# Column-tiled dense matmuls beside PV, V expanded by DMA, and joined ln/exp in a fused attention and token-mixer kernel

## The chip, the cores and the metric

The kernel runs on one core of one Trainium2 chip. The metric is device time in microseconds (us), the median of several executions. "PE" is the matmul engine, "PEld" its weight loads, "DVE" the vector engine, "ACT" the scalar (activation) engine, "POOL" the general engine, "SP" the engine that issues DMAs. The times of one kernel lie within about 1% of each other. So a difference of 2 us between two kernels is near the edge of what these runs can tell.

## The reference

Two layers. Each is attention with a sliding window of 256 over 2,048 tokens with 32 heads of 16 elements, then a mixer that multiplies along the tokens.

```python
# attention: B=1, S=2048, D=512, H=32, Dh=16, W=256
q, k, v = split(layernorm(x) @ wqkv)
scores = einsum("bhqd,bhkd->bhqk", q, k) * Dh ** -0.5
p = softmax(where(0 <= q_idx - k_idx < 256, scores, -1e9))
x = x + (p @ v merged over the heads) @ wo
# token mixer: F=1792
u = gelu(einsum("bsd,sf->bdf", layernorm(x), w1) + b1)     # u is [D, F]
x = x + (einsum("bdf,fs->bds", u, w2) + b2) transposed
# both once more with the same weights
```

## The kernel before

The program builds a graph of operations. A small list scheduler with assumed costs orders them for each engine, at build time; the chip then runs five fixed instruction streams that wait for each other on semaphores.

Scores ("sc") take 32 of PE's 128 rows for each of four heads. PV takes 32 of PE's columns for each of four groups of heads. Everything else (projections, output projection, both halves of the mixer) is "dense", on the whole array; V's projection uses 64-column tiles. Dense groups ("fillers", class "f") are put between scores and PV, so that PE has work while ACT takes the exp.

```python
LAT = {...}; SWITCH = 95.0            # assumed cost of a change of tiling on PE
def _rank(self, o, now, ready):       # who goes first on PE among those that can start
    ...
    if o.cls == "sc":   k = 0
    elif o.cls == "pv": k = 1 if self.cfg in ("sc", "pv") or now - ready[o.idx] > 2500 else 3
    else:               k = 2         # fillers
    return (k, o.prio, o.idx)

# PSUM: 3 pairs of banks for scores, and 2 single banks
psum2 = Pool("psum2", 3)
psum  = Pool("psum", 2)
psum.classes = {"od": [0, 1], "f": [0, 2]}   # od: what PV sums into; f: fillers

# a dense group: matmuls into one bank, which DVE then copies out
def proj(o, which):
    ft = filler(wide)
    mm_group(ft, 4, lambda e, c: e.matmul(bank(ft), lhsT=wqkv[:, c, ...], rhs=xhT[:, tx.slot, c, :], ...))
    op("vector", lambda e: e.tensor_copy(qT[...] or stg[...], bank(ft)), ...)

# V: projection in 64-column tiles, copy by DVE, expansion to block-diagonal form by POOL
for h in range(2):
    op("gpsimd", lambda e, h=h: e.tensor_scalar(vbd[:, tk.slot, 2*sp:2*sp+2, :, 16*h:16*h+16],
       stg[...], half[:, h:h+1], 0.0, op0=ALU.mult, op1=ALU.add), ...)

# attention: scores -> exp (ACT) -> mask (DVE) -> PV (PE) -> denominators
last = e.matmul(bank(t)[32*r:32*r+32, ...], lhsT=onesbd[:] if den else vbd[:, tk.slot, jj, 4*o + r, :],
                rhs=pt[:, tp.slot, r, ...], tile_position=(0, 32*r), ...)
# per group of 8 heads: DVE copies out, ACT takes exp(-ln(denominator)), POOL multiplies
op("scalar", lambda e: e.activation(rl[:, tr.slot, 1, :], rl[:, tr.slot, 1, :], ACTF.Ln), ...)              # 256 columns
op("scalar", lambda e: e.activation(rl[:, tr.slot, 1, :], rl[:, tr.slot, 1, :], ACTF.Exp, scale=-1.0), ...)
```

The softmax here doesn't subtract the row's maximum and nothing guards it: scores larger than these inputs give would overflow.

Of the kernel before, what the change touches and what calls it, by code (L numbers as in the profile page):

```python
# [6 lines left out]
dt = mybir.dt  # L7
ALU = mybir.AluOpType
# [27 lines left out]
class Op:  # L36
    __slots__ = ("idx", "eng", "fn", "cost", "lat", "prio", "deps", "users", "ndeps", "tiles", "start", "end",
                 "done", "seq", "dma", "extra", "cfg", "cls")


class Graph:
# [13 lines left out]
    def op(self, eng, fn, reads=(), writes=(), cost=100.0, lat=None, prio=None, dma=False, after=(), holds=(),  # L55
           cfg=None, cls=None):
# [5 lines left out]
        o.cfg, o.cls = cfg, cls  # L62
# [80 lines left out]
    LAT = {"tensor": 205.0, "vector": 125.0, "scalar": 155.0, "gpsimd": 95.0, "sync": 0.0}  # L143
    SWITCH = 95.0

    def _rank(self, o, now, ready):
        if o.cls is None:
            return (0, o.prio if o.prio is not None else o.idx, o.idx)

        if o.cls == "sc":  # L150
            k = 0
        elif o.cls == "pv":
            k = 1 if self.cfg in ("sc", "pv") or now - ready[o.idx] > 2500 else 3
        else:
            k = 2
        return (k, o.prio, o.idx)

    def schedule(self):
        self.cfg = None
# [4 lines left out]
        dma_free = 0.0  # L164
# [5 lines left out]
        while left:  # L170
            best = None
            for e in self.ENGS:
                m = INF
                ests = []
                for o in cand[e]:
                    t = max(ready[o.idx], free[e])
                    if any(tl.slots is None for tl in o.tiles):
                        t = max(t, self._alloc_time(o))
                    ests.append(t)
                    if t < m:  # L180
                        m = t
# [9 lines left out]
            if o.dma:  # L191
                free[e] = m + 600.0
# [3 lines left out]
            else:  # L196
                if e == "tensor":
                    if o.cfg != self.cfg:
                        o.cost += self.SWITCH
                    self.cfg = o.cfg  # L200
                o.end = free[e] = m + o.cost
                o.done = o.end + o.lat
# [12 lines left out]
    def emit(self, block):  # L215
# [60 lines left out]
        for e in self.ENGS:  # L276
            def body(eng, e=e):
                for o in self.order[e]:
                    for s, v in waits[o.idx]:
                        eng.wait_ge(sem(s), v)  # L280
                    ins = o.fn(eng)
# [47 lines left out]
def bass_interleave_layers__sliding_block__mixer_token_mlp__prompt_kernel(  # L329
# [22 lines left out]
    with es:  # L352
# [9 lines left out]
        vbd = sb("vbd", [P, 3, 8, 16, 32])  # L362
        pt = sb("pt", [P, NPT, 4, 512])
        rl = sb("rl", [P, 4, 2, 256], dt.float32)
# [28 lines left out]
        p_kv, p_pt, p_rl, p_oT = Pool("kv", 3), Pool("pt", NPT), Pool("rl", 4), Pool("oT", 3)  # L393
# [66 lines left out]

        def ln_stats(t):
# [5 lines left out]
        def ln_block(t, twice):  # L467
# [9 lines left out]
               reads=[f"x{t}", f"ag{t}", f"rs{t}"], writes=[f"xh{t}"], cost=dve_cost(512, 0.25, ptrs=2))  # L477
# [9 lines left out]

        def mm_group(dst, n, mk, reads, cols=512, step=2, prio=None, holds=(), after=()):

            prio = fprio() if prio is None else prio  # L490
            for k0 in range(0, n, step):
                k1 = min(n, k0 + step)

                def f(e, k0=k0, k1=k1):
                    last = None
                    for k in range(k0, k1):
                        last = mk(e, k)
# [3 lines left out]
                   cls="f")  # L501


        def qkv(m, wide0):
            tx, tq, tk = Tile(p_xhT), Tile(p_qT), Tile(p_kv)
            wide = wide0
            for i in range(4):
                t = 4 * m + i
                if not wide:
                    op("sync", lambda e, i=i, t=t: e.dma_start_transpose(xhT[:, tx.slot, :, i * P:(i + 1) * P],  # L510
                                                                         xh_sb[:, t, :]),
                       reads=[f"xh{t}"], writes=[(tx, i)], dma=True, cost=900, prio=-1e5)
# [17 lines left out]
            def proj(o, which):  # L530
                ft = filler(wide)
                ts = Tile(p_stg) if which else None
                mm_group(ft, 4, lambda e, c: e.matmul(  # L533
                    bank(ft), lhsT=wqkv[:, c, which * 512 + o * P:which * 512 + (o + 1) * P],
                    rhs=xhT[:, tx.slot, c, :], start=(c == 0), stop=(c == 3)), XT + [f"w{which}"],
# [7 lines left out]
                for h in range(2):  # L543
                    op("gpsimd", lambda e, h=h: e.tensor_scalar(  # L544
                        kbd[:, tk.slot, o, :, h, :], stg[:, ts.slot, :].rearrange("p (s n) -> p s n", n=64),
                        par[:, h:h + 1], 0.0, op0=ALU.mult, op1=ALU.add),
                       reads=[ts, ("par", h)], writes=[(tk, "k", o, h)], cost=pool_cost(512, 1))

            def vproj(sp):
                ft, ts = filler(wide), Tile(p_stg)  # L550
                for k0 in range(0, 4, 2):
                    def f_v(e, k0=k0):
                        last = None
                        for c in range(k0, k0 + 2):
                            for sc in range(2):
                                tok = (2 * sp + sc) * 64
                                for hf in range(2):
                                    last = e.matmul(
                                        bank(ft)[64 * hf:64 * hf + 64, sc * 256:(sc + 1) * 256],
                                        lhsT=xhT[:, tx.slot, c, tok:tok + 64],  # L560
                                        rhs=wqkv[:, c, 1024:1536].rearrange("p (r h e) -> p r h e", h=2, e=16)[:, :, hf, :],
                                        start=(c == 0 and sc == 0), stop=(c == 3), tile_position=(0, 64 * hf),
                                        skip_group_check=True)
                        return last
                    op("tensor", f_v, reads=[(tx, sp), "w2"], writes=[ft], cost=mm_cost(4, 256),
                       prio=fprio(), holds=[ts, tk], cfg="v", cls="f")
                op("vector", lambda e: e.tensor_copy(stg[:, ts.slot, :], bank(ft)),  # L567
                   reads=[ft], writes=[ts], cost=dve_cost(512, psum=True), prio=-2e5)
                for h in range(2):
                    op("gpsimd", lambda e, h=h: e.tensor_scalar(  # L570
                        vbd[:, tk.slot, 2 * sp:2 * sp + 2, :, 16 * h:16 * h + 16],
                        stg[:, ts.slot, :].rearrange("p (s r e) -> p s r e", s=2, e=16), half[:, h:h + 1], 0.0,
                        op0=ALU.mult, op1=ALU.add),
# [17 lines left out]
        def attention(c, tqs, tks):  # L591
# [6 lines left out]
            for o2 in range(0, 4, 2):  # L598
# [3 lines left out]
                od = {}  # L602
                left = {o2: nb, o2 + 1: nb}
                for su in order:
# [3 lines left out]
                    def f_sc(e, su=su, tt=(tA, tB)):  # L608
                        last = None
                        for k, o, base in su:  # L610
                            for j, q0, n, c0 in plan[k][0]:
                                tk, jj = blk(j)
                                for r in range(4):
                                    last = e.matmul(  # L614
                                        PS[:, 2 * tt[r // 2].slot + r % 2, base + c0 * 64:base + (c0 + n) * 64],
                                        lhsT=kbd[32 * r:32 * r + 32, tk.slot, o, jj, :, :].rearrange("p h n -> p (h n)"),
# [8 lines left out]
                    prev_sc[0] = op("tensor", f_sc, reads=rd, writes=[tA, tB], cost=cols / 2.4 + 15,  # L625
# [7 lines left out]
                    for c0, nc_, w0 in plan[su[0][0]][1]:  # L633
# [8 lines left out]
                        op("vector", f_mask, reads=keys + LD, writes=keys, cost=dve_cost(4 * n * nc_ * 64, 0.5))  # L642
                    for k, o, base in su:
# [4 lines left out]
                        def f_pv(e, k=k, o=o, base=base, tp=tp, first=first, t=od[o]):  # L648
                            last, st = None, first
                            for j, q0, n, c0 in plan[k][0]:  # L650
                                tk, jj = blk(j)
                                for den in (0, 1):
                                    for r in range(4):
                                        last = e.matmul(  # L654
                                            bank(t)[32 * r:32 * r + 32, den * 256 + q0 * 64:den * 256 + (q0 + n) * 64],
                                            lhsT=onesbd[:] if den else vbd[:, tk.slot, jj, 4 * o + r, :],
# [8 lines left out]
                        op("tensor", f_pv, reads=keys + rd, writes=[od[o]], cost=plan[k][2] * 128 / 2.4 + 15,  # L665
# [4 lines left out]
                        t, tr = od[o], Tile(p_rl)  # L670
                        op("vector", lambda e, t=t, tr=tr: e.tensor_copy(  # L671
# [183 lines left out]
```

## Time and profile before

| | before |
|---|---|
| time | 504.44 us (503.77 to 505.47, 4 runs) |
| span of the profiled run, granted clock of PE | 503.9 us, 0.996 |
| PE / DVE / ACT / POOL busy | 94% / 71% / 68% / 40% |
| attention of layer 1, first to last exp of the scores | 16.7 to 181.9 us |
| attention of layer 2 | 230.7 to 412.0 us |

The busy share is a mean over stages. The last 92 us, after the last exp, are dense matmuls alone.

Groups of instructions of the kernel before that the change touches (busy us, mean ns of one, then idle time before them and what ended it):

```profile
L676 ACT ACTIVATE rl<-rl 128x256 f32<-128x256 f32 x64 | 29.5, 461 | 0.3
L674 ACT ACTIVATE rl<-rl 128x256 f32<-128x256 f32 x64 | 29.3, 458 | 11.2 <-DVE rl L671 11.0
L654 PEld LDWEIGHTS PS<-pt,vbd 128*32 128x32 bf16 x1920 | 44.1, 96 | 39.3 <-DVE pt L638 14.2 <-issue 5.7 <-DVE agg L464 3.2
L654 PE MATMUL PS<-pt,vbd 128*32 128x64 bf16 x480 | 17.0, 199 | 0.7 <-DVE pt L640 0.6
```

### The profile page before, as it was taken

To read this page: it belongs to the slowest core of one execution; us is meant where nothing else is said; L and a number is where in the kernel's file an instruction comes from. 1 tells how busy PE (TensorE), PEld (TensorE's weight loads), DVE (VectorE), ACT (ScalarE), POOL (GpSimd) and SP (SyncE) were. 2 spreads that over 40 slices of the span, in tenths; PEclk is the share of its full clock that TensorE was granted. 3 is DMA by queue.
4 is the path that set the end of the run, shared out by engine and by line. 5 is a ranking of instruction groups with operands and counts; after the bars stand their busy time and mean duration, and the time that the engine had idled before them with its cause. 6 is when DMAs were issued, how large, how long until landed. Compare 5 with 4: busy or idle time off the path is not lost.

```text
span 503.9 us, 16930 instructions
## 1 busy us (share of the span) xinstructions
PE 471.2 (94%) x7584; PEld 231.2 (46%) x7584; DVE 357.8 (71%) x715; ACT 342.6 (68%) x464; POOL 202.0 (40%) x330
## 2 busy tenths in 40 slices
PE   3977989999999999999999999999989899999997
PEld 1553445545444444453454445344544444444443
DVE  6898998887867755477778878887888685342222
ACT  1597999999999964404993999399979980330000
POOL 3797876666213221036427535643655131000000
PEclk9998999999999999999999999999999999999999
DMA  8411120330131377410030034700100239534163
GB/s 266 80 34 34 24 34 3 84 88 3 44 86 46 86 187 198 113 38 12 3 97 12 14 86 96 178 3 14 23 2 3 77 107 255 142 100 140 56 197 102
DMA packets 81689, 39.89 MB, mean 79 GB/s; under 512 B 18128, under 2 KB 81616, under 8 KB 81616
## 3 DMA queue, kind: packets, MB, share of 16 engines
q1 hardware_dynamic: 81616, 38.81, 29.3%
q8 instruction: 59, 0.97, 0.8%
q14 instruction: 14, 0.11, 0.1%
HBM read 33.56 MB, written 2.10 MB: 71 GB/s over the span
## 4 chain that ended last, share of the span: by engine, by line
PE 45%; ACT 31%; DVE 18%; POOL 4%; issue 1%; DMA 1%
ACT pt L628 27%; PE PS L780 16%; PE PS L754 10%; PE PS L740 5%; PE PS L654 5%; DVE pt L638 3%; PE PS L533 3%; PE PS L614 3%; DVE stats L462 3%; PE PS L687 2%; DVE xh_sb L475 2%; ACT rl L674 2%; DVE stg L567 2%; ACT rl L676 2%; DVE qT L538 2%; DVE rl L671 1%
## 5 line engine op out<-in xcount | busy, mean ns | idle before, releaser
L628 ACT ACTIVATE pt<-PS 128x1024 bf16<-128x1024 f32 (+1 forms) x304 | 295.3, 1058 | 55.4 <-PE PS L614 54.5
L638 DVE TENSOR_TENSOR pt<-pt,ldm 128x512 bf16<-128x512 bf16 (+1 forms) x192 | 77.0, 401 | 24.9 <-ACT pt L628 23.1
L654 PE MATMUL PS<-pt,vbd 128*32 128x64 bf16 (+3 forms) x1920 | 82.8, 237 | 7.1 <-DVE pt L638 4.7
L678 POOL TENSOR_TENSOR oT<-rl 128x256 bf16<-128x256 f32 x64 | 48.1, 751 | 91.7 <-ACT rl L676 91.1
L654 PE MATMUL PS<-pt,onesbd 128*32 128x64 bf16 (+3 forms) x1920 | 81.8, 233 | 0.0
L533 PE MATMUL PS<-xhT,wqkv 128*128 128x512 bf16 x256 | 67.0, 392 | 2.8 <-DVE stg L541 0.9
L780 PE MATMUL PS<-uT,w2b 128*128 128x512 bf16 x280 | 65.8, 380 | 0.8 <-DVE rl L671 0.8
L614 PE MATMUL PS<-qT,kbd 32*128 32x64 bf16 (+3 forms) x1920 | 60.6, 232 | 4.1 <-ACT pt L628 2.3
L544 POOL TENSOR_SCALAR kbd<-stg,par 128x512 bf16<-128x512 bf16 x64 | 51.2, 811 | 27.6 <-DVE stg L541 23.8
L654 PEld LDWEIGHTS PS<-pt,vbd 128*32 128x32 bf16 x1920 | 44.1, 96 | 39.3 <-DVE pt L638 14.2
L740 PE MATMUL PS<-xh_sb,w1b 128*128 128x512 bf16 x224 | 55.1, 381 | 1.7 <-DVE w2b L744 0.8
L570 POOL TENSOR_SCALAR vbd<-stg,half 128x512 bf16<-128x512 bf16 x64 | 50.4, 799 | 13.1 <-DVE stg L567 8.4
L614 PEld LDWEIGHTS PS<-qT,kbd 32*128 32x128 bf16 x1920 | 27.6, 93 | 57.5 <-ACT pt L628 37.6
L785 DVE SCALAR_TENSOR_TENSOR x_sb<-PS,b2col,x_sb 128x512 bf16<-128x512 f32 x32 | 24.0, 749 | 39.7 <-PE PS L780 39.7
L754 PE MATMUL PS<-xh_sb,w1b 128*128 128x512 bf16 x224 | 49.2, 379 | 0.8 <-DVE x_sb L690 0.8
L770 ACT ACTIVATE uT<-rl,b1col 128x512 bf16<-128x512 f32 x28 | 18.4, 712 | 44.5 <-DVE rl L764 44.5
L471 POOL TENSOR_SCALAR rstd<-agg 128x1 f32<-128x1 f32 x64 | 13.6, 213 | 82.7 <-DVE agg L464 79.9
L654 PEld LDWEIGHTS PS<-pt,onesbd 128*32 128x32 bf16 x1920 | 45.8, 97 | 0.1
L671 DVE COPY rl<-PS 128x512 f32<-128x512 f32 x64 | 43.6, 681 | 2.9 <-PE PS L654 2.3
L462 DVE BATCH_NORM_STATS2 stats<-x_sb 128x6 f32<-128x512 bf16 x64 | 43.7, 686 | 1.3 <-DMA x_sb<-in_A_x_dram 0.4
L473 POOL TENSOR_TENSOR rstd<-rstd,mhalf 128x1 f32<-128x1 f32 x64 | 39.0, 610 | 3.8
L475 DVE TENSOR_SCALAR xh_sb<-x_sb,agg,rstd 128x512 bf16<-128x512 bf16 x64 | 32.9, 515 | 10.4 <-POOL rstd L473 9.6
(45 smaller groups left out, 487.6 us busy)
## 6 DMA issues: line engine op xcount, KB each, us to landing
w1b<-in_B_w_dram SPq DMA_DIRECT2D x28, 512.0 KB, 4.7
w2b<-in_B_w_dram SPq DMA_DIRECT2D x10, 896.0 KB, 5.2
pt<-in_B_w_dram SPq DMA_DIRECT2D x12, 448.0 KB, 6.5
out_dram<-x_sb SPq DMA_DIRECT2D x16, 128.0 KB, 1.8
wqkv<-in_A_wqkv_dram SPq DMA_DIRECT2D x3, 512.0 KB, 6.2
x_sb<-in_A_x_dram SPq DMA_DIRECT2D x3, 512.0 KB, 8.8
x_sb<-in_A_x_dram SPq DMA_DIRECT2D x2, 256.0 KB, 3.0
wo_sb<-in_A_wo_dram SPq DMA_DIRECT2D x1, 512.0 KB, 8.9
```

The lines of the kernel that those rows point to most:

```text
L462: op("vector", lambda e: e.bn_stats(stats[:, t, :], x_sb[:, t, :]), reads=[f"x{t}"], writes=[f"st{t}"], cost=dve_cost(512))
L533: mm_group(ft, 4, lambda e, c: e.matmul(bank(ft), lhsT=wqkv[:, c, which * 512 + o * P:which * 512 + (o + 1) * P], rhs=xhT[:, tx.slot, c, : ...
L544: op("gpsimd", lambda e, h=h: e.tensor_scalar(kbd[:, tk.slot, o, :, h, :], stg[:, ts.slot, :].rearrange("p (s n) -> p s n", n=64), par[:, ...
L570: op("gpsimd", lambda e, h=h: e.tensor_scalar(vbd[:, tk.slot, 2 * sp:2 * sp + 2, :, 16 * h:16 * h + 16], stg[:, ts.slot, :].rearrange("p ( ...
L614: last = e.matmul(PS[:, 2 * tt[r // 2].slot + r % 2, base + c0 * 64:base + (c0 + n) * 64], lhsT=kbd[32 * r:32 * r + 32, tk.slot, o, jj, :, ...
L628: op("scalar", lambda e, ts=ts, tp=tp, i=i, cols=cols: e.activation(pt[:, tp.slot, 2 * i:2 * i + 2, 0:cols], PS[:, 2 * ts.slot:2 * ts.slot ...
L638: return e.tensor_tensor(v, v, msk.unsqueeze(1).to_broadcast([P, 4, w]), op=ALU.mult)
L654: last = e.matmul(bank(t)[32 * r:32 * r + 32, den * 256 + q0 * 64:den * 256 + (q0 + n) * 64], lhsT=onesbd[:] if den else vbd[:, tk.slot, j ...
L671: op("vector", lambda e, t=t, tr=tr: e.tensor_copy(rl[:, tr.slot].rearrange("p a b -> p (a b)"), bank(t)), reads=[t], writes=[tr], cost=dv ...
L740: mm_group(ft, 8, lambda e, sc, tt=tt, ft=ft: e.matmul(bank(ft), lhsT=w1b[:, tw.slot, sc, tt * P:(tt + 1) * P], rhs=xh_sb[:, sc, :], start ...
L754: last = e.matmul(PS[:, 2 * tu.slot + tt, :], lhsT=w1b[:, tw.slot, sc - 8, tt * P:(tt + 1) * P], rhs=xh_sb[:, sc, :], start=(sc == 8), sto ...
L780: mm_group(ft, NFT, lambda e, fc: e.matmul(bank(ft), lhsT=w(fc)[:, k * P:(k + 1) * P], rhs=uT[:, fc, :], start=(fc == 0), stop=(fc == NFT ...
```

## The change

PE should change its tiling less often, ACT should do fewer instructions, POOL should lose most of V's expansion. The core of the diff:

```diff
# 1. dense matmuls next to sc or pv become four 32-column tiles; V's projection too (cfg "v" -> "pv")
+        def matmul(e, cols32, o, w, x, start, stop):
+            if not cols32:
+                return e.matmul(o, lhsT=w, rhs=x, start=start, stop=stop, skip_group_check=True)
+            for j in range(0, P, 32):
+                last = e.matmul(o[j:j + 32], lhsT=w[:, j:j + 32], rhs=x, start=start, stop=stop,
+                                tile_position=(0, j), skip_group_check=True)
+            return last
+                    if o.flex and self.cfg in ("sc", "pv"):      # in the scheduler
+                        o.cfg = "pv"
# 2. V: columns of one head 16 elements apart, so that a DMA moves runs of 512 bytes; zeroed once by POOL
+        for i in (1, 2):
+            op("gpsimd", lambda e, i=i: e.memset(<vbd slot i, 128x4096 bf16 as 128x2048 f32>, 0.0), ...)
+                        op("sync", lambda e, h=h: e.dma_start(<vbd half h>, <stg half h>), ...)   # 48 of 64
-  lhsT=onesbd[:] if den else vbd[:, tk.slot, jj, 4 * o + r, :],
+  lhsT=onesbd[:] if den else vbd[:, tk.slot, jj, 4 * o + r::16],
# 3. ln and exp of the denominators once for two groups of heads
-                        op("scalar", ... rl[:, tr.slot, 1, :] ... Ln)      # 256 columns, 64 times; Exp the same
+                        for fn, sc in ((ACTF.Ln, 1.0), (ACTF.Exp, -1.0)):
+                            op("scalar", ... rl[:, tr.slot, 1] ...)        # 512 columns, 32 times each
# 4. a new order: rank of PV, more costs in the scheduler's model
-            k = 1 if self.cfg in ("sc", "pv") or now - ready[o.idx] > 2500 else 3
+            k = 1 if self.last == "pv" or now - ready[o.idx] > 2500 else 3
... (in the scheduler's model: lock of the port that DVE and POOL share, cold clock at the start, issue time of DMAs;
     also 3 rl buffers of twice the size in place of 4, and the last output projection of a layer in a single bank)
```

A reason for the strided weights in 2: a version that read two runs of 16 columns did not build.

## The prediction

> **What bounds it now.** The page gives PE 94% busy, DVE 71%, ACT 68%, POOL 40% of 503.9 us. The chain of waits names ACT (31%, mostly the scores' exp) between 80 and 165 us and between 327 and 410 us, but I do not take it for the limit. After each stretch PE still works off dense matmuls that did not fit (first-half w1 until 180 and 428 us, then 24 us of w1 and 48 us of w2 at 216 ns per 512-column matmul). So the time is PE's work plus PE's lost time. From the timeline's start times: streaming all columns at 2.4 GHz, four at a time where 32-wide tiles are used, needs about 398 us. The other 106 us are lost, about 95 of them between groups of different tiling. There are some 450 changes of group (score rows, PV columns, V columns, dense), median 115 to 140 ns above streaming each: about 55 us. The other 40 us are waits, 12 of them between 20 and 80 us (windows: DVE 19 of each 20 us, POOL up to 19).
>
> The Trainium skill (TensorEngine Tiling (Array Packing), Key Properties) says that changing the tiling mode drains the engine; the 115 to 140 ns at each change agree.
>
> **What the change does.**
> 1. Dense matmuls next to PV, and V's projection, use PV's column tiling, so PV-dense and PV-V changes no longer drain. What stays is about two changes for each of the 152 score groups, some 300 in place of 450: 150 x 125 ns, about -18 us, all on PE. Four 32-wide matmuls should stream like one dense one: PV's four 256-column matmuls already start every 109 ns. They lose fast weight load (same page), but PV's weight loads hide at this pitch. I allow +3 us.
> 2. 48 of 64 V expansions (799 ns) leave POOL: -38 us of 202, plus 4 for zeroing. They become 48 small DMAs of about 2 to 3 us with slack, since K and V are made a block ahead. The chain is little on POOL (4%): perhaps -4 us of PE waits, early and between 225 and 325 us.
> 3. 128 ln/exp of 256 columns (458 and 461 ns) become 64 of 512, about 670 ns (256 columns more at 0.83 ns): ACT -16 us of 343. ACT being half hidden, -3 us of PE waits.
> 4. The new order lets fillers run ahead of PV: fewer waits behind exp and mask, -3 us. Strided V weights and V copy cost +1 us.
>
> Sum: -18 + 3 - 4 - 3 - 3 + 1 = -24 us: **480 us**, range 467 to 493. Faster by over 2%: 0.84; within 2%: 0.12; slower: 0.04.
>
> **What would show it.** PE starts after PV-dense changes at streaming pitch, with about 300 drains of 115 to 140 ns left; dense matmuls of 32 columns four to about 216 ns; POOL near 165 us; ln and exp 32 each near 670 ns; ACT near 327 us; the last 72 us unchanged; the gain spread over 20 to 428 us.
>
> **What would make it wrong.** Column-tiled dense matmuls slower than 216 ns for four (weight loads showing): 740 groups x 30 ns would eat all. The V DMA stuck behind transposes on its in-order queue, so that PV waits. PV delayed so long that the probability buffers run out and ACT stalls. A much slower strided V copy on DVE, which is full between 20 and 60 us. The other way: more of the 40 us of waits gone.

## More of the kernel before

The page of the kernel before: busy time by engine, the instruction queue, and the chain of waits (the work that ended last, followed backwards), by engine and by line. L628 is the exp of the scores.

```profile
PE 471.2 (94%) x7584; PEld 231.2 (46%) x7584; DVE 357.8 (71%) x715; ACT 342.6 (68%) x464; POOL 202.0 (40%) x330
...
q8 instruction: 59, 0.97, 0.8%
...
PE 45%; ACT 31%; DVE 18%; POOL 4%; issue 1%; DMA 1%
ACT pt L628 27%; PE PS L780 16%; PE PS L754 10%; PE PS L740 5%; PE PS L654 5%; DVE pt L638 3%; PE PS L533 3%; PE PS L614 3%; DVE stats L462 3%; PE PS L687 2%; DVE xh_sb L475 2%; ACT rl L674 2%; DVE stg L567 2%; ACT rl L676 2%; DVE qT L538 2%; DVE rl L671 1%
```

PE is the busiest engine, but the chain runs through ACT for 31% of the span. Two stretches of the kernel before in the windows view (start and end, length, then busy us of PE, PEld, DVE, ACT and POOL with counts, granted clock, DMA share, GB/s):

```profile
56.00:140.00 84.00, 79.81 (x1785) 41.53 (x1786) 72.49 (x142) 81.66 (x109) 51.96 (x75) 1.00 0.18 42
140.00:180.00 40.00, 39.44 (x856) 19.27 (x852) 29.36 (x60) 40.00 (x56) 9.34 (x16) 1.00 0.23 66
```

Between 140 and 180 us ACT never pauses (40.00 of 40.00 us) and PE is busy 39.44. But in the 124 us of these two lines ACT is idle for 84.00 − 81.66 = 2.34 us in all. At this order, and with the same work on ACT, nothing that is done to PE can make this stretch shorter by more. In layer 2 it is different: between 231 and 410 us the same view leaves ACT idle for 22.7 us.

## The result

| | before | after |
|---|---|---|
| time | 504.44 us (503.77 to 505.47, 4 runs) | 510.14 us (507.39 to 510.57, 4 runs) |
| profiled span, granted clock | 503.9 us, 0.996 | 508.4 us, 0.993 |
| first matmul | 6.8 us | 9.3 us |
| attention of layer 1 (first to last exp) | 165.2 us long | 167.9 us long |
| attention of layer 2 | 181.2 us long | 180.9 us long |

The ratio after to before is 1.010, with a 95% interval of 1.006 to 1.014. Here and below a ratio is the mean time of one kernel's runs over that of the other's in the same rounds, so it is not quite the ratio of the medians. The change costs 1%, where 24 us of gain were predicted. The page of the kernel after, the same lines (L662 is the scores' exp; L510 are the column-tiled dense matmuls, L508 and L791 the others):

```profile
PE 464.8 (91%) x10334; PEld 252.7 (50%) x10334; DVE 357.2 (70%) x715; ACT 337.4 (66%) x400; POOL 168.3 (33%) x284
...
q8 instruction: 81, 1.33, 1.0%
...
PE 55%; ACT 23%; DVE 19%; issue 1%; POOL 1%; POOLq 0%
ACT pt L662 22%; PE PS L510 17%; PE PS L508 13%; PE PS L791 9%; PE PS L689 8%; PE PS L648 4%; PE PS L582 3%; DVE stats L479 3%; DVE pt L672 3%; DVE xh_sb L492 2%; DVE rl L706 2%; DVE pt L674 2%; ACT rl L712 2%; DVE stg L591 2%; DVE x_sb L728 2%
```

POOL lost what was predicted (202.0 to 168.3 us), but ACT only 5 us and not 16, and PE went from 7,584 to 10,334 matmuls. The windows view of the kernel after, the same two stretches of time (not quite the same work):

```profile
56.00:140.00 84.00, 77.69 (x2360) 46.09 (x2360) 70.05 (x141) 80.80 (x94) 36.40 (x54) 1.00 0.24 55
140.00:180.00 40.00, 38.35 (x1112) 21.14 (x1108) 28.73 (x59) 39.83 (x48) 8.83 (x15) 1.00 0.25 70
```

PE's busy time fell from 39.44 to 38.35 us in the second stretch. ACT is still at 39.83 of 40. The groups of the kernel after:

```profile
L689 PEld LDWEIGHTS PS<-pt,vbd 128*32 128x32 bf16 x1920 | 64.7, 139 | 26.9 <-DVE pt L672 6.3 <-DVE pt L674 3.3 <-issue 2.5
L712 ACT ACTIVATE rl<-rl 128x512 f32<-128x512 f32 x64 | 42.2, 659 | 15.1 <-DVE rl L706 14.9
L689 PE MATMUL PS<-pt,vbd 128*32 128x64 bf16 x480 | 19.8, 223 | 2.3 <-DVE pt L674 1.1 <-DVE uT L781 0.4 <-DVE x_sb L728 0.4
```

### A ledger of PE

From the start times of all matmuls: streaming every column at 2.4 GHz, four tiles at a time where tiles are used, needs 398 us in both kernels. What lies between first and last matmul beyond that is lost time. I count a gap at a change of tiling as a drain of about 105 ns and what is beyond (over 150 ns) as a wait.

| us | before | after |
|---|---|---|
| first to last matmul | 493.5 | 495.6 |
| changes of tiling | 466 | 307 |
| drains (about 105 ns each) | 49 | 32.5 |
| waits beyond | 31.7 | 41.0 |
| PV slowed by strided weights | – | 6.3 |

The rest, about 15 and 18 us, is a few nanoseconds at each step within a group. So 159 changes went, 9 more than predicted, with their 16.5 us. Four 32-column matmuls of 512 columns start 216 ns after the four before them, like one dense matmul (medians; the means in the kernel after are 217.9 and 216.0). Both were right. The gain came back as waits and as slower PV. Of the waits before, 22.0 us end with work of DVE (masks, copies, normalisation) and 3.3 with work of ACT; after, 24.7 and 5.7. The waits also hold dense matmuls that run at half rate, 427 ns in place of 216: about 3.2 us before and 2.5 us after, at the start or just after PE has stood still. (Records of some matmuls are missing from a few of the traces below, so below I count drains only in the pair whose records are complete; for the others the drains are changes of tiling times 105 ns.)

### Four costs that the traces show

**Start.** DVE in the timeline of the kernel before (start us, length us, engine, line, operation):

```profile
2.43 0.18 DVE L444 CAST onesbd<-half 128x32 bf16<-128x32 f32 x1
2.52 0.23 DVE L450 TENSOR_SCALAR ldm<-tri,half 128x64 bf16<-128x64 bf16 x1
```

The same two instructions in the timeline of the kernel after, and the second of POOL's two new fills:

```profile
2.44 3.10 DVE L454 CAST onesbd<-half 128x32 bf16<-128x32 f32 x1
2.53 3.03 DVE L460 TENSOR_SCALAR ldm<-tri,half 128x64 bf16<-128x64 bf16 x1
...
3.69 1.81 POOL L474 MEMSET vbd<- 128x2048 f32 x1
```

A cast of 32 columns takes 3.10 us in place of 0.18, and ends as POOL's fill ends (3.69 + 1.81 = 5.50). The Trainium skill, "SBUF — State Buffer", section "Who interferes with whom", says that DVE (in a mode that uses two ports) and POOL share a port pair as an exclusive lock, and that the later one blocks fully. The trace agrees that DVE stands still while POOL fills, and with the fills moved to ACT (run a_zero_act, below) the same cast takes 0.18 us again. One thing is not as on the page, which gives the pair to whoever issues first: the cast began at 2.44 us, before the second fill at 3.69, and still waited for both. The first matmul moves from 6.8 to 9.3 us.

**Strided weights.** The weight loads of V take 139 ns in place of 96, and the 64-column matmuls that follow 223 in place of 199.

**Late instructions.** PE and its weight loads in the timeline of the kernel after, inside one PV group:

```profile
263.62 0.23 PE L689 MATMUL PS<-pt,onesbd 128*32 128x128 bf16 x3
266.12 0.22 PE L689 MATMUL PS<-pt,onesbd 128*32 128x128 bf16 x1 [2.28 <-issue]
266.12 0.36 PEld L510 LDWEIGHTS PS<-wo_sb,oT 128*32 128x32 bf16 x12 [2.46 <-issue]
```

Three of four equal matmuls have run; the fourth, which waits for no other engine, comes 2.5 us later. The instruction queue moved 59 packets of 16 KB before and 81 after. Before this pause no packet had been fetched for 466 PE instructions (matmuls and weight loads), where about 250 is usual; one started at 263.4 us, while a load of 896 KB of w2 and three V transfers were under way. Pauses of this kind sum to 4.9 us (1.3 us at 107.7, 2.4 here, 0.9 at 313.8, 0.3 at 318.5), against none before. The second and third longest follow stretches of 461 and 354 instructions without a packet. That PE waits for its instructions is an inference from this; no run tests it alone.

A pause has an after-effect: from 267.5 us the granted clock was 0.5 for 3.4 us, and six dense groups took 427 ns each in place of 216. The kernel before shows the same at 39.1 us, behind a wait of 2.2 us for POOL. The mean granted clock of a run tells how many such stretches it had, and slower runs go with more of them: the kernel before took 503.76 to 504.52 us at 1.0 (13 runs) and 505.65 to 505.89 at 0.993 (4 runs). The kernel after never ran above 0.993, so an estimated 1.3 us of its 5.7 us go with the lower clock (against the four runs at 0.993).

**Overlap on ACT.** ACT in the timeline of the kernel before, in its saturated stretch:

```profile
129.04 1.07 ACT L628 ACTIVATE pt<-PS 128x1024 bf16<-128x1024 f32 x1
129.94 0.48 ACT L674 ACTIVATE rl<-rl 128x256 f32<-128x256 f32 x1
130.25 1.08 ACT L628 ACTIVATE pt<-PS 128x1024 bf16<-128x1024 f32 x1
131.15 0.48 ACT L676 ACTIVATE rl<-rl 128x256 f32<-128x256 f32 x1
131.46 2.92 ACT L628 ACTIVATE pt<-PS 128x1024 bf16<-128x1024 f32 x3
```

The same of the kernel after:

```profile
138.73 0.64 ACT L712 ACTIVATE rl<-rl 128x512 f32<-128x512 f32 x1
139.25 1.04 ACT L662 ACTIVATE pt<-PS 128x1024 bf16<-128x1024 f32 x1
140.15 0.66 ACT L712 ACTIVATE rl<-rl 128x512 f32<-128x512 f32 x1
```

Each instruction starts before the last has ended. From start to start, ln costs 130.25 − 129.94 = 0.31 us, not 0.48, and the joined one 139.25 − 138.73 = 0.52, not 0.66. So joining saves 128 × 0.306 − 64 × 0.520 = 39.2 − 33.3 = 6 us, not 16 (0.306 and 0.520 are the usual back-to-back distances). The Trainium skill, "ScalarE: Activation LUTs", section "What ACT_TABLE_LOAD costs", gives 186 ns + 0.833 ns per column for an ACTIVATE and an overlap of about 93 ns. An estimate from these figures is 186 + 213 − 93 = 306, and 186 + 427 − 93 = 520. For ln and exp of the denominators the trace agrees to the nanosecond; I had used durations. For the exps of the scores, which read 1,024 columns from PSUM, the same estimate is 186 + 853 − 93 = 946, and there the trace decides: 904 to 905 ns from start to start.

### The profile page after: what moved, and what is told of

It reads as the page before. It is cut to its first block, busy times and chain, and to the rows that moved or that the text cites. A ratio compares the mean times of both kernels' runs of the same rounds, so it can differ in the third digit from the quotient of the medians.

```text
span 508.4 us, 22384 instructions
## 1 busy us (share of the span) xinstructions
PE 464.8 (91%) x10334; PEld 252.7 (50%) x10334; DVE 357.2 (70%) x715; ACT 337.4 (66%) x400; POOL 168.3 (33%) x284
## 4 chain that ended last, share of the span: by engine, by line
PE 55%; ACT 23%; DVE 19%; issue 1%; POOL 1%; POOLq 0%
ACT pt L662 22%; PE PS L510 17%; PE PS L508 13%; PE PS L791 9%; PE PS L689 8%; PE PS L648 4%; PE PS L582 3%; DVE stats L479 3%; DVE pt L672 3%; DVE xh_sb L492 2%; DVE rl L706 2%; DVE pt L674 2%; ACT rl L712 2%; DVE stg L591 2%; DVE x_sb L728 2%
## 5 line engine op out<-in xcount | busy, mean ns | idle before, releaser
L662 ACT ACTIVATE pt<-PS 128x1024 bf16<-128x1024 f32 (+1 forms) x304 | 287.1, 1046 | 62.3 <-PE PS L648 54.5
L689 PE MATMUL PS<-pt,vbd 128*32 128x64 bf16 (+3 forms) x1920 | 88.2, 251 | 6.0 <-DVE pt L672 3.2
L689 PEld LDWEIGHTS PS<-pt,vbd 128*32 128x32 bf16 x1920 | 64.7, 139 | 26.9 <-DVE pt L672 6.3
L510 PE MATMUL PS<-xhT,wqkv 128*32 128x512 bf16 x960 | 61.7, 381 | 5.8 <-DVE qT L563 2.7
L510 PE MATMUL PS<-xh_sb,w1b 128*32 128x512 bf16 x896 | 56.8, 380 | 0.5 <-DVE rl L706 0.3
L689 PEld LDWEIGHTS PS<-pt,onesbd 128*32 128x32 bf16 x1920 | 51.5, 106 | 4.0 <-issue 1.4
L712 ACT ACTIVATE rl<-rl 128x512 f32<-128x512 f32 x64 | 42.2, 659 | 15.1 <-DVE rl L706 14.9
L791 PE MATMUL PS<-xh_sb,w1b 128*128 128x512 bf16 x224 | 49.2, 379 | 1.9 <-DVE xh_sb L492 1.9
L510 PE MATMUL PS<-uT,w2b 128*32 128x512 bf16 x560 | 36.2, 388 | 0.2
L582 PE MATMUL PS<-wqkv,xhT 128*32 128x256 bf16 x1024 | 34.1, 273 | 2.5 <-DVE stg L591 1.8
```

Source lines behind the costliest of these rows:

```text
L510: last = e.matmul(o[j:j + 32], lhsT=w[:, j:j + 32], rhs=x, start=start, stop=stop, tile_position=(0, j), skip_group_check=True)
L582: last = e.matmul(bank(ft)[32 * j:32 * j + 32, sc * 256:(sc + 1) * 256], lhsT=xhT[:, tx.slot, c, tok + 32 * (j % 2):tok + 32 * (j % 2) + 3 ...
L662: op("scalar", lambda e, ts=ts, tp=tp, i=i, cols=cols: e.activation(pt[:, tp.slot, 2 * i:2 * i + 2, 0:cols], PS[:, 2 * ts.slot:2 * ts.slot ...
L689: last = e.matmul(bank(t)[32 * r:32 * r + 32, den * 256 + q0 * 64:den * 256 + (q0 + n) * 64], lhsT=onesbd[:] if den else vbd[:, tk.slot, j ...
L712: op("scalar", lambda e, tr=tr, fn=fn, sc=sc: e.activation(rl[:, tr.slot, 1], rl[:, tr.slot, 1], fn, scale=sc), reads=[(tr, 0), (tr, 1), " ...
L791: last = e.matmul(PS[:, 2 * tu.slot + tt, :], lhsT=w1b[:, tw.slot, sc - 8, tt * P:(tt + 1) * P], rhs=xh_sb[:, sc, :], start=(sc == 8), sto ...
```

## The experiments

Kernels of one batch share a chip and the runs of the kernel before. The theories, in the order in which they came up:

- ACT's theory: in the attention stretches ACT sets the pace, so drains saved on PE become waits there.
- The theory of added costs: the change brought costs (start, strided weights, late instructions) that ate a real gain.
- The order's theory: the new order is worse than the old one.
- The bank's theory, which came late: the fillers' single PSUM bank, emptied by DVE, paces the kernel next after ACT.

The texts of expectation were written batch by batch, and their numbers and letters hold only there. In the batches before the last two, "theory A" is ACT's (with DVE), "theory B" is the prediction's (PE is the limit throughout), "theory O" is the order's, "theory 1" of the first batch is that the tiles do what was predicted, and "theory 2" or "C" is a hidden cost of the column tiles. In the last two batches, "theory 1" is ACT's, "theory 2" is that PE loses its gain again on PE itself (late instructions, weight loads), and "theory 3" is the bank's. A run "at the same order" was checked: the traces show DVE, ACT and POOL doing the same operations in the same sequence as in the kernel that it is compared with, up to the fills that were added or moved.

### Each part in the order of the kernel after

The dense matmuls issued 128 wide again, at the same order:

```diff
-                    ins = o.fn(eng, o.cfg == "pv") if o.flex else o.fn(eng)
+                    ins = o.fn(eng, False) if o.flex else o.fn(eng)
```

> The changed kernel in its own order on every engine, but with every dense matmul issued as one 128-wide matmul again (V's projection stays at four column tiles). Theory 1 (column tiling does what was predicted, and its gain is eaten elsewhere): about 150 more drains of 105 ns, +16 us, less some 5 us because PE has a third fewer instructions to fetch: 519 to 523 us against 510. Theory 2 (column-tiled dense matmuls carry a hidden cost of their own that cancels the drains, in instruction fetch or weight loads): within 3 us of 510, and PE's waits put down to 'issue' fall from 6.7 us to about 2.

Measured: 513.03 us (512.14 to 514.25), ratio to before 1.016. In this order the tiles bring 2.9 us, where PE has 424 changes of tiling in place of 307, an estimated 117 × 105 ns = 12 us. This is within the bound of that text's theory 2 (3 us), but not its reason: a pause of PE of 1.9 us is left, behind a stretch of 497 instructions without a packet, although only 63 packets were fetched in all.

PV reads the contiguous columns of V, with the rest unchanged (wrong, relative error 1.7):

```diff
-  vbd[:, tk.slot, jj, 4 * o + r::16]
+  vbd[:, tk.slot, jj, 32 * (4 * o + r):32 * (4 * o + r) + 32]
```

> The changed kernel in its own order, wrong results on purpose: PV loads 32 neighbouring columns of V in place of 32 columns that lie 16 elements apart. Theory 1 (the strided weight load lengthens PV): PV's V groups of 64 and 128 columns lose their 31 ns each, about 6 us of PE, so 503 to 506 us. Rival (PE waits for other engines and the slower PV hides in these waits): within 2 us of 510.

Measured: 507.90 us (505.89 to 510.16), ratio 1.006. The weight loads of V are back at 97 ns. The stride costs 2.2 us of time by the medians (6.3 us on PE's ledger, so most of it in slack). The intervals of the two ratios overlap (1.006 to 1.014 and 1.003 to 1.009), so the size is uncertain by about as much.

The zero fills on ACT, which has nothing to do at the start:

```diff
-  op("gpsimd", lambda e, i=i: e.memset(<vbd slot i>, 0.0), ..., cost=1900, prio=1e3)
+  op("scalar", lambda e, i=i: e.activation(<vbd slot i>, ident[:, 0:1].to_broadcast([P, 4096]), ACTF.Copy, scale=0.0), ...)
```

> The changed kernel in its own order, with the two zero fills of V's buffers (1.81 us each) taken from POOL and done by ACT, which is idle at the start. Theory 1 (the fills hold up DVE's set-up instructions, 3.1 and 3.0 us long in place of 0.2, and with them the first normalisation and the first matmul): the first matmul starts near 7 us in place of 9.3, total 507 to 508.5 us. Rival (the start is made up later, since PE is not the limit before 40 us): within 1 us of 510.

Measured: 507.58 us (504.77 to 510.16), ratio 1.005, first matmul at 6.9 us. The fills cost 2.6 us by the medians, with the same uncertainty; the first matmul is earlier by 2.4.

### The change, mended

V's columns now lie 4 elements (8 bytes) apart, heads in groups of four, so that the DMA still moves runs of 128 bytes; and the zero fills are on ACT. The Trainium skill, "SBUF — State Buffer", section "Specifications (TRN2)", says that SBUF has lines of 16 bytes and needs two or more hits on each for full bandwidth: 32 bytes apart is one hit a line, 8 bytes apart is two.

```diff
-  vbd[:, tk.slot, jj, 4 * o + r::16]
+  vbd[:, tk.slot, jj, 128 * o + r:128 * o + 128:4]
```

> The changed kernel in its own order on every engine, results correct: V's 32 columns lie 4 elements apart in place of 16 (heads in groups of four, so the DMA moves runs of 128 bytes in place of 512), and the zero fills are ACT's. If the two costs measured singly (2.4 us for the fills, 2.2 us for the strided weights) add up and the short stride costs nothing, 505 to 506.5 us; if a stride of 8 bytes costs as much as one of 32 bytes, 507 to 508.

Measured: 504.72 us (502.42 to 506.88), ratio 0.999, correct. The two losses add up (2.2 + 2.6 = 4.8; measured 5.4, which is clear of the noise). The weight loads of V take 108 ns and the 64-column matmuls 201, which fits the page's rule except for some 11 ns of each load. Mended, the change is worth nothing: the theory of added costs explains why it got slower, not where 24 us went.

### Column tiles alone, in the order of the kernel before

The tiling is chosen after scheduling, so that every engine keeps its order:

```diff
+        for o in self.order["tensor"]:
+            if o.flex:
+                o.cols32 = mode in ("sc", "pv")
+            mode = "pv" if o.cfg in ("pv", "v") or (o.flex and o.cols32) else o.cfg
-  (V's projection in 64-column tiles)
+  (V's projection in 32-column tiles)
```

> The kernel before in its own order on every engine, with only this of the change: dense matmuls that follow scores or PV, and V's projection, issued as four column tiles. Theory 1: the drains between PV and dense go, 466 tiling changes become about 300 at 105 ns, so -13 to -17 us, less 3 to 5 us for more instruction fetch: 490 to 494 us. Theory 2 (hidden cost of column-tiled dense matmuls): 502 to 508 us.

Measured: 505.85 us (505.43 to 507.09), ratio 1.002. PE has 311 changes of tiling in place of 466, drains fall by 16 us, and waits rise by 14.7 us. The time meets that text's theory 2, but not its reason, since the column-tiled groups start every 216 ns like the others. The windows view of this run, the two stretches of layer 1:

```profile
56.00:140.00 84.00, 78.65 (x2360) 43.02 (x2360) 72.50 (x142) 81.25 (x109) 51.70 (x75) 1.00 0.18 42
140.00:180.00 40.00, 38.73 (x1116) 20.41 (x1112) 29.39 (x60) 40.00 (x55) 9.28 (x16) 1.00 0.24 67
```

ACT is as full as before, and PE less. Comparing the start of every exp with the kernel before: over exps 80 to 120 of 304 (106.9 to 148.7 us) the distance stays within 0.04 us, although PE has 40 changes of tiling there in place of 60; over exps 200 to 216 it stays within 0.03 us, with 16 in place of 24. In the first of these the kernel before lets ACT stand still only once, for 0.31 us, so ACT sets the pace there. In other stretches the distance moves, by up to 2.4 us in layer 1 and 1.7 in layer 2.

### ACT and masks lighter

ln and exp of the denominators and the masks work on 2 columns (wrong), same order; without and with the tiles.

```diff
-  e.activation(rl[:, tr.slot, 1, :], rl[:, tr.slot, 1, :], ACTF.Ln)
+  e.activation(rl[:, tr.slot, 1, 0:2], rl[:, tr.slot, 1, 0:2], ACTF.Ln)        # Exp the same
-  def f_mask(e, tp=tp, n=n, c0=c0, w=nc_ * 64, w0=w0):
+  def f_mask(e, tp=tp, n=n, c0=c0, w=2, w0=w0):
```

> The kernel before in its own order on every engine, wrong results on purpose: the ln and exp of the denominators work on 2 columns in place of 256 and the masks on 2 columns in place of up to 384, so ACT loses some 30 us and DVE some 50 us of work, PE none. It is the base for the run with column tiles added. Theory A (in the attention stretches PE keeps step with ACT and DVE through a fixed order, so removed drains turn into waits): 15 to 30 us faster than before, 475 to 490. Theory B (PE is the limit throughout, as predicted): at most 8 us faster.

Measured: 490.40 us (489.80 to 491.12), ratio 0.972.

> The same lightened ACT and DVE, with the column tiles of the run b_cols. Theory A: with ACT and DVE out of the way the 155 removed drains show: 9 to 16 us faster than the lightened kernel without column tiles. Theory C (column-tiled dense matmuls carry a cost of their own, such as instruction fetch, that cancels the drains whatever the other engines do): within 3 us of it, and most of PE's waits are put down to 'issue'.

Measured: 489.42 us (489.18 to 490.08), ratio 0.970. PE's work is the same in the first of the two as before, and 14 us are gone: PE was not the limit of those 14. (Whether ACT or the masks on DVE were is not told apart here.) But the tiles bring only 1 us even now, where theory A of that text wanted 9 to 16, so ACT and the masks alone are not enough.

### ACT far lighter

The exps of the scores write half their columns as well. The probability buffers are filled with ones at the start, by POOL; that moves the first matmul from 6.8 to 14.9 us in both kernels of the pair.

```diff
-  pt[:, tp.slot, 2*i:2*i+2, 0:cols], PS[:, 2*ts.slot:2*ts.slot+2, 0:cols], ACTF.Exp
+  pt[:, tp.slot, 2*i:2*i+2, 0:cols // 2], PS[:, 2*ts.slot:2*ts.slot+2, 0:cols // 2], ACTF.Exp
```

> The kernel before, at its own order, made far lighter on ACT (wrong on purpose): the exps of the scores write half their columns, ln, exp of denominators and masks work on two columns; the probability buffers are filled with ones at the start. If ACT's exp sets the pace of the attention stretches, this must shorten them much more than the 14 us of the run with light ln/exp and masks: 465 to 478 us, with PE over 0.97 busy in the attention stretches. If PE already was the limit in most of the time, it stays at 484 to 490 us.

Measured: 497.99 us (497.80 to 498.11). Less the later start (8.1 us) that is 489.9, no better than the 490.4 with full exps. ACT's share fell from 65% to 41% of the span and the time did not move: once ln, exp and masks are light, ACT is not the limit, although it was 96% busy from 56 to 140 us before the exps were cut (80.65 of 84 us in the windows view of the run before).

> The same as the kernel with half exps, and dense matmuls beside PV and V's projection as four column tiles (same order). Theory 1 (the saved drains were hidden because ACT sets the pace): with ACT out of the way the tiles now bring most of their 16 us of drains, so 10 to 16 us less than the kernel with half exps. Theory 2 (what the tiles save in drains they lose again on PE itself, in late instructions and weight loads): within 4 us of the kernel with half exps.

Measured: 494.47 us (493.71 to 494.94). The tiles bring 3.5 us, which meets theory 2 as it was put there and not theory 1. The timeline of this kernel shows the next pacer. PE's groups (L502 dense, L631 scores, L671 PV), and DVE's copy out of the dense group's bank:

```profile
108.65 1.03 PE L502 MATMUL PS<-xhT,wqkv 128*32 128x512 bf16 x16
109.62 0.40 PE L631 MATMUL PS<-qT,kbd 32*128 32x192 bf16 x12
109.74 0.69 DVE L558 CAST stg<-PS 128x512 bf16<-128x512 f32 x1 [0.26 <-PE PS L502]
109.95 0.27 PE L671 MATMUL PS<-pt,vbd 128*32 128x192 bf16 x4
...
110.34 0.23 PE L671 MATMUL PS<-pt,onesbd 128*32 128x128 bf16 x4
110.48 0.83 PE L502 MATMUL PS<-xhT,wqkv 128*32 128x512 bf16 x12
```

The dense group starts at 108.65, its copy at 109.74, the copy ends at 109.74 + 0.69 = 110.43, and the next dense group starts at 110.48. The loop through this one bank takes 110.48 − 108.65 = 1.83 us. PE had finished streaming PV 86 ns earlier: of the 108 ns (median) that the drain takes from PV to dense without tiles, most have become this wait. This is one step; how many are like it is counted below. The Trainium skill, "Perfetto Trace Analysis", section "Matmuls" under "Optimizing Tensor Performance", advises that independent groups rotate through different banks so that emptying one overlaps the next group; with "od" taken, two banks leave no rotation.

### Banks emptied early as well

Every DVE instruction that empties a bank of PE's work takes 2 of 512 columns (wrong; more buffers filled with ones, first matmul at 21.9 us in both).

```diff
-  e.tensor_copy(qT[:, tq.slot, o, :], bank(ft))
+  e.tensor_copy(qT[:, tq.slot, o, 0:2], bank(ft)[:, 0:2])      # k, v, output projection, mixer, denominators the same
```

> The kernel with half exps, and also every DVE instruction that empties a PSUM bank of PE's work (q, k, v, output projection, mixer sums, denominators) cut to 2 of 512 columns, so that the banks come free about 0.6 us earlier (wrong on purpose; buffers filled with ones at the start, which adds some 15 us at the start to this kernel and the next alike). Its own time decides nothing; it is the base of the next one.

Measured: 491.78 us (491.62 to 492.58).

> The last one with the dense matmuls beside PV and V's projection as four column tiles, same order. Theory 3 (what the tiles save on PE is taken back by the wait for the one PSUM bank that dense groups have while PV holds the other: dense group 0.86 us, 0.2 us to DVE, copy 0.69 us, so about 1.83 us, as long as a whole period of 1.85 us): with the banks free early, the tiles now bring 10 to 16 us (3.5 us with half exps alone), and gaps between PV and dense of the same tiling are at 2 to 3 ns nearly everywhere. Theory 2 (PE loses it to late instructions and weight loads): still within 5 us.

Measured: 482.85 us (482.07 to 484.06). Now the tiles bring 8.9 us, more than theory 2 allowed and a little less than theory 3 wanted. The windows view of the first of the two, the stretch from 140 to 180 us: PE is busy all the time, ACT and DVE are far from it.

```profile
140.00:180.00 40.00, 40.00 (x863) 19.59 (x863) 11.59 (x62) 23.14 (x56) 8.77 (x16) 1.00 0.24 69
```

Weight loads of the projections' column tiles with half exps alone, by what ended the idle time before them:

```profile
L502 PEld LDWEIGHTS PS<-xhT,wqkv 128*32 128x32 bf16 x960 | 21.5, 96 | 24.6 <-DVE qT L555 3.2 <-DVE rl L688 2.5 <-DVE stg L558 1.9
```

The same group with the banks emptied early:

```profile
L507 PEld LDWEIGHTS PS<-xhT,wqkv 128*32 128x32 bf16 x960 | 23.0, 96 | 18.9 <-issue 0.8 <-DVE stg L563 0.2
```

The waits for DVE are nearly gone. Of 90 steps from PV to column-tiled dense, 87 now take 2 to 3 ns beyond streaming (57 of 90 with half exps alone). The ledger of this pair closes: drains (gaps up to 160 ns) 47.1 to 31.9 us, −15.2; waits over 150 ns 6.9 to 13.2 us, +6.3, of which pauses that nothing in the profile explains 0 to 4.7 and waits for a transposing DMA 0.6 to 2.6; sum −8.9. The run can't tell an early bank from a lighter DVE: the same edit took DVE from 60% to 36% of the span.

The four pairs together. The time of each is the median less the start of the first matmul in its profiled run, so that the fills at the start don't count:

| same order of all engines | without tiles | with tiles | tiles bring |
|---|---|---|---|
| as before | 504.44 − 6.8 = 497.6 | 505.85 − 6.7 = 499.2 | +1.5 |
| ln, exp of denominators and masks light | 490.40 − 6.7 = 483.7 | 489.42 − 6.6 = 482.8 | −0.9 |
| and half exps | 497.99 − 14.9 = 483.1 | 494.47 − 14.9 = 479.6 | −3.5 |
| and banks emptied early | 491.78 − 21.9 = 469.9 | 482.85 − 21.9 = 461.0 | −8.9 |

Read down the first column: PE's work is the same in all four rows, and the time falls by 28 us. PE was not the limit for those 28 us. Read down the last: the saved drains show only as fast as the other loops are taken away; by layers (first to last exp, layer 1 and 2) the tiles bring +1.2 and +1.3, −2.0 and +0.2, −2.8 and −1.1, −5.0 and −3.6 us. Some 5 us of 15 are still lost in the last row, to pauses put down to late instructions.

### The order

One constant of the scheduler of the kernel before, nothing else:

```diff
-    SWITCH = 95.0
+    SWITCH = 90.0
```

> The kernel before with nothing changed but one constant of its scheduler (a tiling change is charged 90 ns in place of 95), so the same instructions in another order. If the order alone moves the time as much as the whole change did (theory O), over 4 us away from 504.4 either way, more likely slower, since the order of before was picked; if orders are equivalent, within 2 us.

Measured: 514.26 us (513.96 to 515.54), ratio 1.019. The same work in another order is 10 us slower, with 469 changes of tiling against 466.

Another order of the kernel before, chosen by replaying its scheduler with many constants:

```diff
-    SWITCH = 95.0
+    SWITCH = 124.0
-  k = 1 if self.cfg in ("sc", "pv") or now - ready[o.idx] > 2500 else 3
+  k = 1 if self.cfg == "pv" or now - ready[o.idx] > 3492 else 3
```

> The kernel before with only the order made anew by the new rule for PV (PV follows PV, and otherwise goes behind dense work until it has waited 3.5 us) and 124 ns charged for a tiling change; no column tiles, no other part of the change. Theory O: a better order without any new instruction can beat before, 496 to 502 us. If only fewer drains help, 503 to 512.

Measured: 504.48 us (504.00 to 504.62), ratio 0.999.

Two parts alone, with the order made anew. First the tiles, of which the scheduler now knows, with the old rank of PV:

```diff
+                    if o.flex and self.cfg in ("sc", "pv"):
+                        o.cfg = "pv"                       # no change of tiling is counted
-                    ins = o.fn(eng)
+                    ins = o.fn(eng, o.cfg == "pv") if o.flex else o.fn(eng)
```

> The kernel before with the column tiles and with the scheduler told of them (a dense matmul after scores or PV takes PV's tiling, and only real tiling changes are charged), so that the order is made anew with the old rule for PV. Theory A: a new order can put other work into the freed time, but ACT and DVE have as much to do as before, so 0 to 8 us faster than before, 496 to 504. Theory B: the full 13 to 16 us, 488 to 491.

Measured: 516.99 us (516.83 to 517.60), ratio 1.025; its PE waits 12.4 us for masks on DVE, against 5.4 us in the kernel before. Why is not shown: PV follows scores directly 103 times, against 102 before.

Then the joined ln/exp (part 3 of the change) and nothing else:

```diff
-  rl = sb("rl", [P, 4, 2, 256], dt.float32)
+  rl = sb("rl", [P, 3, 2, 2, 256], dt.float32)
-  (Ln and Exp on 256 columns for each group of 8 heads)
+  (Ln and Exp on 512 columns for each two groups)
```

> The kernel before with only the ln and exp of denominators joined for sixteen heads, order made anew. ACT's work falls by 16 us of 343. Theory A: half of that lies where ACT sets the pace, so 4 to 9 us faster, 495 to 500. Theory B: 0 to 3 us faster.

Measured: 515.71 us (515.29 to 516.01), ratio 1.022, with one pause of ACT of 14.8 us near 325 us. These two do not measure their part. Each holds a new draw of the order as well, and one constant alone moved the order's time by 10 us.

Both of these together on the kernel before, POOL's V kept, with an order chosen by replay:

```diff
-    SWITCH = 95.0
+    SWITCH = 118.0
-  k = 1 if self.cfg in ("sc", "pv") or now - ready[o.idx] > 2500 else 3
+  k = 1 if self.cfg == "pv" or now - ready[o.idx] > 1414 else 3
```

> The kernel before with column tiles and joined ln and exp, V still expanded by POOL in the old layout, so neither the fills nor the strided weights, and an order made for it with the new kind of rule for PV. If the change's two good parts are worth something once the order suits them, 494 to 501 us; if column tiles give nothing in any order, 503 to 510.

Measured: 507.79 us (506.59 to 510.80), ratio 1.006. The attempt failed.

The mended change with two other orders, again by two constants alone:

```diff
-    SWITCH = 95.0
+    SWITCH = 102.0                                                              # second: 106.0
-  k = 1 if self.last == "pv" or now - ready[o.idx] > 2500 else 3
+  k = 1 if self.last == "pv" or now - ready[o.idx] > 3746 else 3                # second: 3603
```

> The mended change (V columns 8 bytes apart, zero fills on ACT; correct) with the scheduler's constants 102 and 3746 in place of 95 and 2500, so only another order. If the mended change is held back mainly by its order, 498 to 503 us (504.7 with the first order); if every order meets ACT as the limit, 504 to 508.

Measured: 503.34 us (501.86 to 504.88), ratio 0.996.

> As the last one, with constants 106 and 3603: again an order alone. Same two expectations: 498 to 503 us if the order holds it back, 504 to 508 if not. The spread between the two shows how far an order's draw goes in this kernel.

Measured: 501.45 us (500.43 to 502.69), ratio 0.993 with an interval of 0.991 to 0.995, correct. It beats both kernels, by 0.7% and 1.7%. It does not come near the predicted 480.

## Why the prediction was wrong

**"I do not take it for the limit" (ACT) and "the time is PE's work plus PE's lost time": this step failed.** PE was the busiest engine, and its ledger of lost time was right. But an engine's lost time is not what it can win. In the attention stretches, where a pair of exps is one round, three loops run side by side. ACT's takes two exps of 0.904 us and its share of ln and exp, 128 × 0.306 / 152 = 0.26 us: 2.07 us. PE's takes about 1.86 us (the usual distance where the banks are emptied early and PE never pauses), with 0.31 us of drains in it. The fillers' bank takes 1.83 us. The kernel before needed 165.2 / 76 = 2.17 us for a round of layer 1. Taking 0.1 us out of PE's 1.86 cannot shorten a round that ACT makes 2.07 long; and with ACT light it can shorten it only to the bank's 1.83, an estimated 152 × 0.03 = 4.6 us (measured with half exps: 3.5). The chain of waits had pointed there, with ACT at 31% of the span and 27% at one line. I set it aside because PE finished dense work after each stretch. The table of four pairs shows the step wrong: +1.5 us with all loops in place, −8.9 us with two of them cut.

This sum of loops fits layer 1 alone. In layer 2 a round took 181.2 / 76 = 2.38 us, more than any of the three, and even with all else cleared away it takes 167.6 / 76 = 2.21, longer than ACT's. The tiles brought nothing there either (181.2 to 182.5 us), so the step failed in layer 2 too, but which loop took the gain is not explained.

**The drains, "150 x 125 ns, about -18 us, all on PE".** The count (159) and the dense rate (216 ns for four) were right; the size was 105 ns each, 16.5 us. "On PE" was true and "on the critical path" was not. The page that I cited for the drain, "TensorEngine Tiling (Array Packing)", says in its section "PSUM Bottleneck" that tiling speeds up PE but not the emptying of PSUM, whose copy may then be the limit. The timeline with half exps shows one such step, 0.69 us of copy in a loop of 1.83.

**The weight loads, "I allow +3 us".** Right, and small. But 2,750 more matmuls bring more instructions to fetch (59 to 81 packets), and that term was missing: pauses of 4.9 us in the kernel after and none before, 4.7 us and none in the pair where all else was cleared away. That these pauses are fetches come late is inferred.

**V's expansions off POOL, −4 us.** POOL fell as predicted and the V transfers (2.6 us each, at most 6.2) held up no PE group that the trace names. But the zero fills at the start, counted as 4 us of POOL, held DVE and so PE: +2.6 us. I had costed them on the engine that does them and not on the one they block.

**ln and exp, "ACT -16 us of 343", −3 us.** The term of ACT was mis-sized: 6 us by distance from start to start, 5 us in busy time. A round of ACT falls from 2.07 to 2.03 us by it. What it brings alone at a fixed order was not measured.

**"Strided V weights and V copy cost +1 us".** Measured +2.2 us for the weights, within the noise of either figure.

**The new order, −3 us.** Not a term that can be added. One constant moves the kernel before by +10 us, and two constants move the mended change by −3.3 us. Of the two other orders of the kernel before that were tried, one was equal and one slower, so its order looks like a good draw, which a change of the graph gives up.

Sum as measured: fills +2.6, stride +2.2, all the rest together about 0 (the mended change at 504.72 against 504.44). That rest is a sum of gains and losses (drains, ln and exp, pauses, clock, order) that no run separates.

What stays open: what paces layer 2 and takes the tiles' gain there; how the 14 us of the lighter kernel divide between ACT and the masks on DVE; whether the last 5.4 us of the tiles (8.9 less 3.5) come from early banks or from a lighter DVE; whether the pauses are late instructions; what joined ln/exp brings at a fixed order; and what a third bank for fillers would bring, since all eight banks are in use and a kernel with one more was not built.

## What to carry to other kernels

When two engines are each over 95% busy in a stretch, removing lost time from one of them need not bring anything: find every loop with nearly the same period (each engine's start-to-start distances, and each buffer's fill, wait and emptying), and count only the slack to the next one. Test "on the critical path" by lightening the other engines at the same order, as the four pairs do, before building the improvement. And in a kernel whose order a scheduler makes, hold the order fixed when measuring a part: here one constant of the scheduler was worth 10 us, more than any part of the change brought.

## What the Trainium skill lacked or had wrong

- No page has pauses for instruction fetch on PE as a cost of more, smaller matmuls. "Runtime: NRT & Kernel Launch", section "Instruction fetch mechanics", calls the cost of a new block of instructions mostly hidden. Runs: 59 to 81 packets of 16 KB, pauses of PE up to 2.4 us in the middle of a group that waits for nothing else, 4.9 us in sum (that they are fetches is inferred; belongs also to "TensorEngine Tiling (Array Packing)", section "Instruction Overhead").
- "TensorEngine Tiling (Array Packing)", "Key Properties", says that a change of mode drains PE, but not for how long. Runs: 99 ns from dense to scores, 101 to 102 from scores to PV, 108 from PV to dense (medians); and 2 to 3 ns from PV to dense in the same column tiling.
- The same page, "Restrictions" under "Tile-to-Partition Mapping", says that column tiling disables fast weight load, which reads as a cost. Runs: four column-tiled matmuls of 512 columns take as long as one dense one, 216 ns (medians; 217.9 and 216.0 in the mean).
- "SBUF — State Buffer", "Specifications (TRN2)", gives two hits per 16-byte line as a rule without a size for weight loads. Runs: weights of 32 columns take 96 ns contiguous, 108 ns at 8 bytes apart, 139 ns at 32 bytes apart.
- "ScalarE: Activation LUTs", "What ACT_TABLE_LOAD costs": the estimate from its figures for back-to-back ACTIVATEs meets the ln and exp of the denominators (306 and 520 ns), but not exps of 1,024 columns read from PSUM: 946 ns, and the runs show 904 to 905.
- "SBUF — State Buffer", "Who interferes with whom": the port lock agrees with the traces, except for who goes first. Runs: a DVE cast that began at 2.44 us waited for a POOL fill that began at 3.69.
